# Column-major u, z and result, z's halves swapped by DMA, and a half chunk of keys held twice, in a TensorE-heavy attention and MLP kernel

## The chip, the cores and the metric

The kernel runs on one core of a Trainium2 chip. The metric is the device time of one execution in microseconds; a version is judged by the median of several runs. The profile comes from one execution of its own, recorded by the hardware profiler. Its span is shorter than the time of a run by what lies around it.

## What is computed

Two batches of 3008 rows go through an attention without softmax, and the 6016 rows of its result through two MLPs, one after the other:

```python
def _attn_ref(u, v, z):                     # u, v: [2, 3008, 256]; z: [2, 3008, 64]
    scores = (1.0 / S) * np.matmul(z, z.transpose(0, 2, 1))
    attn = np.maximum(scores, 0.0) ** 2
    return u * np.matmul(attn, v)

def _moe_ref(x, w_in, w_out, a, b):         # w_in: [256, 2048], w_out: [2048, 256]
    h = x @ w_in
    P = a[0] + a[1] * h + a[2] * h**2 + a[3] * h**3
    Q = 1.0 + np.abs(b[0]) * np.abs(h) + np.abs(b[1]) * h**2
    return (P / (Q + 1e-06)) @ w_out

def _moe2_ref(x, w_in, w_out, alpha):       # the same sizes
    h = x @ w_in
    return (np.maximum(h, 0.0) + alpha * np.minimum(h, 0.0)) @ w_out
```

## The kernel before

Products are made in float32 accuracy out of a narrower type, float32r: an operand is cut into a rounded part hi and a rest lo (`split`, line 92: a cast, then a subtraction on VectorE), and hi hi + hi lo + lo hi add up in PSUM. One product of 128 by 128 weights with 512 columns is thus three matmuls.

The 3008 rows of a batch are worked in six blocks of queries, five of 512 and one of 448, twelve blocks in all. Keys come in chunks of 128 partitions, two chunks to a pair, twelve pairs to a block; the last chunk has only 64 keys, and its other 64 partitions are zeros (line 108). Per block:

- `load_z` (line 204) loads 512 rows of z with rows on partitions, splits them on VectorE into a tile [hi | lo] (L96, L97), transposes its four chunks on TensorE (L214, tile zps) and copies the result on ScalarE (L216). That is zA: 64 partitions of hi above 64 of lo. `a_begin` (line 228) makes zB, the same with its halves swapped, by a product with a permutation matrix (L232, tile zbps) and a copy on ScalarE (L234). zA with zA gives hi hi + lo lo of a score, zA with zB gives the two mixed products (L250, L251).
- `a_scores` takes relu (L252) and square (L253) of a pair's scores on ScalarE, and splits them into ahi and alo. In the first block of all VectorE makes both parts, later ScalarE makes ahi.
- `a_values` and `pairs` (line 264) add a pair to the block's sum acca: eight matmuls move hi (v's two parts, two chunks, two halves of the 256 columns; L269), four move lo (L278). They come three pairs after the scores (LAG_A).
- `a_u` and `a_end`, behind a block's last pair: u's rows are loaded into a buffer (uraw), transposed by eight TensorE instructions (L304, tile ups), copied by ScalarE into ut (L307), multiplied with acca on VectorE (L313), and stored to DRAM as xd (L315).

The first MLP (`m1_*`) loads xd of a block (`load_x`, L320), splits it, and works through 2048 hidden units in eight steps of 256: `hidden` (L260 to L262), elementwise work, and `pairs` into acc1. Its result goes to DRAM as x2d (L403); the second MLP (`m2_*`) does the same with x2d. `m2_end` (line 436) copies the sum (L439), transposes it on TensorE (L447, tile ops; eight for a block), copies again (L451, L453) and stores (L455, L459).

What sets the order: 30 steps of attention alone, in which weights of the first MLP are loaded and decoded from float64 words by VectorE (`decode`, line 127); then attention with a share of the first MLP; from about 780 us the two MLPs without attention. The tile framework orders instructions by priorities and dependences, so an engine's list is not the text's order. Each engine works its list in order and waits at an instruction whose inputs are not there.

Shared places: all loads and stores of 4 KB per partition (zraw, vraw, wraw, uraw, ut, xr, x2, ot, o) take turns in two buffers (tag raw, RAW = 2). The tag s, two PSUM buffers, holds scores, the hidden units of the second MLP, and zps, zbps, ups and ops. The tag acc0 holds acca, and later the second MLP's sum. All of these loads and stores are issued by SP in one list (the DMA queue of SyncE; SPq in the rows). The second MLP's prepared weights are fetched by GpSimd's queue (w<-wd, L180), most of them about the end of attention.

## Time and profile before

| | us |
|---|---|
| median of 3 runs | 1631.24 |
| fastest and slowest of them | 1630.53, 1632.41 |
| span of the profiled execution | 1629.7 |
| TensorE matmuls busy | 1595.3 |
| TensorE weight loads busy (beside matmuls) | 1320.9 |
| VectorE busy | 1399.9 |
| ScalarE busy | 1222.4 |
| GpSimd busy | 28.5 |

Busy time of matmuls counts each from its start to its modelled end, and consecutive matmuls overlap. So a share near 98% says that TensorE nearly always has something under way, and what one matmul costs is read from the distance between two starts. The profile names PE for TensorE, PEld for its weight loads, DVE for VectorE, ACT for ScalarE, POOL for GpSimd and SP or SPq for SyncE's DMA queue; L250 is line 250 of the kernel.

### The profile page before, as it was taken

The page shows a single profiled execution, that of the slowest core. Times are in us where ns is not written, and L with a number is a line of the kernel's source. Part 1 is how long each engine was busy: PE and PEld are TensorE (multiplying, and loading weights), DVE is VectorE, ACT ScalarE, POOL GpSimd, SP SyncE. Part 2 cuts the span into 40 slices and gives each one's busy share as a digit, 9 for nine tenths or more (in the row PEclk, how much of TensorE's full clock was granted, in tenths as well). Part 3 has the DMA queues.
Part 4 walks back from the last instruction along what each step waited for, and adds up shares of the span by engine and source line. Part 5 has one row for each costly group of instructions (what it writes and reads, how often), then busy time and mean ns, then how long its engine had stood idle before and what let it go on. Part 6 is the DMA issues. An engine that isn't in the chain of part 4 may idle for free.

```text
span 1629.7 us, 18674 instructions
## 1 busy us (share of the span) xinstructions
PE 1595.3 (98%) x7164; PEld 1320.9 (81%) x7164; DVE 1399.9 (86%) x1498; ACT 1222.4 (75%) x1546; POOL 28.5 (2%) x57
## 2 busy tenths in 40 slices
PE   7899999999999999999899999999999999999998
PEld 5677888888888888888788888888888888888887
DVE  6998898988889888877799898898899989898863
ACT  5688898999989899988567666666666666666643
POOL 0000000000000000001000000000000000000000
PEclk9999999999999999999999999999999999999999
DMA  4323111221112120113400010101101010100000
GB/s 107 103 93 116 56 36 65 81 87 54 52 52 78 52 78 27 52 38 122 146 1 26 25 39 1 39 1 41 49 1 38 1 39 14 37 14 27 14 0 25
DMA packets 48169, 78.51 MB, mean 48 GB/s; under 512 B 9040, under 2 KB 28624, under 8 KB 48080
## 3 DMA queue, kind: packets, MB, share of 16 engines
q1 hardware_dynamic: 41056, 60.53, 11.5%
q0 software_dynamic: 7024, 16.79, 3.4%
q8 instruction: 56, 0.92, 0.2%
q14 instruction: 33, 0.27, 0.1%
HBM read 50.90 MB, written 26.41 MB: 47 GB/s over the span
## 4 chain that ended last, share of the span: by engine, by line
PE 89%; DVE 5%; DMA 2%; ACT 2%; issue 1%; SPq 0%; ACTq 0%; DVEq 0%
PE acc L269 20%; PE acca L269 13%; PE h L260 10%; PE h L261 10%; PE acc L278 10%; PE h L262 10%; PE acca L278 7%; PE s L250 3%; PE s L251 3%; DVE alo L97 1%; DMA vraw<-in_v_dram 1%; PE ops L447 1%; PE ups L304 1%; DMA xr<-xd 1%; DMA wraw<-in_moe_w_in_dram 0%
## 5 line engine op out<-in xcount | busy, mean ns | idle before, releaser
L269 PE MATMUL acc<-ghi,w 128*128 128x512 f32 (+1 forms) x1536 | 378.3, 386 | 0.0
L269 PEld LDWEIGHTS acc<-ghi,w 128*128 128x128 f32 x1536 | 287.7, 188 | 54.0 <-ACT ghi L94 0.3
L260 PE MATMUL h<-xhi,w 128*128 128x512 f32 (+1 forms) x768 | 298.6, 390 | 4.5 <-ACT xhi L94 4.5
L261 PE MATMUL h<-xlo,w 128*128 128x512 f32 (+1 forms) x768 | 297.3, 387 | 0.0
L262 PE MATMUL h<-xhi,w 128*128 128x512 f32 (+1 forms) x768 | 297.3, 387 | 0.0
L269 PE MATMUL acca<-ahi,vt 128*128 128x512 f32 (+1 forms) x1152 | 293.5, 387 | 1.3 <-DVE ut L313 1.1
L269 PEld LDWEIGHTS acca<-ahi,vt 128*128 128x128 f32 x1152 | 215.6, 188 | 44.7 <-DVE ut L313 3.0
L97 DVE TENSOR_TENSOR alo<-r,ahi 128x1024 fp32r<-128x1024 f32 (+1 forms) x144 | 172.6, 1199 | 59.4 <-PE acc L269 46.2
L420 ACT ACTIVATE m<-h,sal 128x512 f32<-128x512 f32 (+1 forms) x192 | 127.8, 680 | 110.7 <-PE h L262 110.1
L369 ACT ACTIVATE sq<-h 128x1024 f32<-128x1024 f32 (+1 forms) x96 | 97.0, 1010 | 141.5 <-PE h L262 139.6
L278 PE MATMUL acc<-glo,w 128*128 128x512 f32 (+1 forms) x768 | 202.8, 385 | 0.2 <-DVE glo L386 0.2
L260 PEld LDWEIGHTS h<-xhi,w 128*128 128x128 f32 x768 | 144.8, 189 | 34.5 <-ACT xhi L94 5.4
L97 DVE TENSOR_TENSOR glo<-m,ghi 128x1024 fp32r<-128x1024 f32 (+1 forms) x96 | 115.2, 1200 | 64.0 <-PE acc L269 48.5
L261 PEld LDWEIGHTS h<-xlo,w 128*128 128x128 f32 x768 | 144.9, 189 | 27.3 <-DVE xlo L97 0.7
L262 PEld LDWEIGHTS h<-xhi,w 128*128 128x128 f32 x768 | 144.9, 189 | 27.0
L278 PEld LDWEIGHTS acc<-glo,w 128*128 128x128 f32 x768 | 144.0, 188 | 27.7 <-DVE glo L386 1.0
L252 ACT ACTIVATE r<-s 128x512 f32<-128x512 f32 (+1 forms) x256 | 143.7, 592 | 23.9 <-DVE t L385 19.1
L421 DVE SCALAR_TENSOR_TENSOR m<-h,sg,m 128x512 f32<-128x512 f32 (+1 forms) x192 | 138.4, 735 | 18.9 <-ACT m L420 18.2
L278 PE MATMUL acca<-alo,vt 128*128 128x512 f32 (+1 forms) x576 | 154.2, 386 | 0.0
L253 ACT ACTIVATE r<-r 128x1024 f32<-128x1024 f32 (+1 forms) x144 | 151.5, 1053 | 2.1
L94 ACT CAST ahi<-r 128x1024 fp32r<-128x1024 f32 (+1 forms) x132 | 135.3, 1032 | 7.4 <-PE acca L278 6.5
L373 DVE SCALAR_TENSOR_TENSOR ab<-sq,cb,ab 128x1024 f32<-128x1024 f32 (+1 forms) x96 | 120.8, 1258 | 15.6 <-ACT ab L370 15.0
(83 smaller groups left out, 2164.2 us busy)
## 6 DMA issues: line engine op xcount, KB each, us to landing
wraw<-in_moe_w_in_dram SPq DMA_DIRECT2D x16, 512.0 KB, 3.7
wraw<-in_moe_w_out_dram SPq DMA_DIRECT2D x16, 512.0 KB, 3.6
wd<-dec POOLq DMA_DIRECT2D x32, 256.0 KB, 2.3
w<-wd POOLq DMA_DIRECT2D x16, 512.0 KB, 3.7
vraw<-in_v_dram SPq DMA_DIRECT2D x10, 512.0 KB, 3.9
uraw<-in_u_dram SPq DMA_DIRECT2D x10, 512.0 KB, 4.0
xd<-ut SPq DMA_DIRECT2D x10, 512.0 KB, 2.8
xr<-xd SPq DMA_DIRECT2D x10, 512.0 KB, 3.2
```

The costliest lines, as they stand in the source:

```text
L94: nc.scalar.copy(dst_hi, src)
L97: nc.vector.tensor_tensor(dst_lo, src, dst_hi.bitcast(F32), ALU.subtract)
L252: nc.scalar.activation(r[:, i, :n], s, AF.Relu, scale=1.0 / S)
L253: nc.scalar.activation(r[:, :, :n], r[:, :, :n], AF.Square)
L260: nc.tensor.matmul(acc, w_hi, hi, start=first, stop=False)
L261: nc.tensor.matmul(acc, w_hi, lo, start=False, stop=False)
L262: nc.tensor.matmul(acc, w_lo, hi, start=False, stop=last)
L269: nc.tensor.matmul(acc[:, e, :n], w[:, k, i, e * P : (e + 1) * P], hi[:, i, :n], start=first and i == 0 and k == 0, stop=False,)
L278: nc.tensor.matmul(acc[:, e, :n], w[:, 0, i, e * P : (e + 1) * P], lo[:, i, :n], start=False, stop=last and i == 1,)
L373: nc.vector.scalar_tensor_tensor(ab, sq, b1, ab, ALU.mult, ALU.add)
L420: nc.scalar.activation(t[:, i], h, AF.Copy, scale=sal[:, f : f + 1])
L421: nc.vector.scalar_tensor_tensor(t[:, i], h, sg[:, f : f + 1], t[:, i], ALU.mult, ALU.max)
```

## The change

The host lays out u as [256, 3008] for each batch, and z as [128, 3008], its 64 rows twice, one below the other. The result leaves the core as [256, 6016], and the host turns it back. Nothing is transposed on TensorE any more, and the identity and the permutation are gone.

`load_z` now gets z column-major: it rounds all 128 partitions into zA, and subtracts on the lower 64 only, in place, so that zA is hi above lo as before. For the first block zB is cut from the same load (ScalarE the lower half, VectorE the upper); for the others `a_begin` makes it by two SBUF-to-SBUF transfers of 64 partitions on SP's queue, which swap zA's halves. `a_u` is one load straight into ut, called once the second-last pair's products are written down. `m2_end` stores the copied sum as it is.

The last chunk of 64 keys is held twice over the partitions, in z's columns and in v's rows. For it the scores' hi stands on partitions 0 to 63 and their lo on 64 to 127 (two subtractions in the last pair); v's lo is set to zero on the lower half. So the passes that moved hi give hi hi + lo hi, and the third pass for this chunk, hi lo, is left out (`both` = 1): the two matmuls, one for each half of the columns.

```diff
+            for p0 in (0, HALF):
+                nc.sync.dma_start(
+                    out=t[p0 : p0 + rest, full, :], in_=src[r0 + full * P : r0 + n, :]
+                )
...
+            if kp + i == NKP - 1:
+
+                h2 = t[HALF:P, 0, 1].bitcast(F32)
+                nc.vector.tensor_tensor(t[HALF:P, 1, 1], h2, h2, ALU.subtract)
...
     def load_z(b, g):
-        """z's rows of one block as [hi; lo] over partitions, transposed."""
+
         raw = raw_tile("zraw")
-        r3 = raw[:, 0 : 4 * DQ].rearrange("p (c d) -> p c d", c=4)
-        load_rows(r3, z[b], g * QB, qn[g])
-        nch = -(-qn[g] // P)
-        zz = zp.tile([P, 4, P], F32R, tag="z", name="zz")
-        split(zz[:, 0:nch, 0:DQ], zz[:, 0:nch, DQ:P], r3[:, 0:nch, :], on_act=False)
-        ps = psw.tile([P, QB], F32, tag="s", bufs=2, name="zps")
-        for c in range(nch):
-            nc.tensor.transpose(ps[:, c * P : (c + 1) * P], zz[:, c, :].bitcast(F32), ident)
+        n = qn[g]
+        nc.sync.dma_start(out=raw[:, 0:n], in_=zt[b, :, g * QB : g * QB + n])
+        if n % P:
+            nc.sync.dma_start(out=raw[:, n : n + HALF], in_=zt[b, :, S - HALF : S])
+            n += HALF
         t = zp.tile([P, QB], F32R, tag="z", name="zA")
-        nc.scalar.copy(t[:, 0 : nch * P], ps[:, 0 : nch * P])
+        nc.vector.tensor_copy(t[:, 0:n], raw[:, 0:n])
+        if (b, g) == (0, 0):
+            zB[b, g] = zp.tile([P, QB], F32R, tag="z", name="zB")
+            nc.scalar.copy(zB[b, g][HALF:P, 0:n], raw[HALF:P, 0:n])
+            nc.vector.tensor_tensor(
+                zB[b, g][0:HALF, 0:n], raw[0:HALF, 0:n], t[0:HALF, 0:n].bitcast(F32), ALU.subtract
+            )
+        nc.vector.tensor_tensor(
+            t[HALF:P, 0:n], raw[HALF:P, 0:n], t[HALF:P, 0:n].bitcast(F32), ALU.subtract
+        )
         zA[b, g] = t
...
     def a_begin(b, j):
+
+        if (b, j) in zB:
+            return
         n = qn[j]
-        ps = psw.tile([P, QB], F32, tag="s", bufs=2, name="zbps")
-        nc.tensor.matmul(ps[:, :n], perm, zA[b, j][:, :n], start=True, stop=True)
         t = zp.tile([P, QB], F32R, tag="z", name="zB")
-        nc.scalar.copy(t[:, :n], ps[:, :n])
+        for p0 in (0, HALF):
+            nc.sync.dma_start(
+                out=t[p0 : p0 + HALF, :n].bitcast(F32),
+                in_=zA[b, j][HALF - p0 : P - p0, :n].bitcast(F32),
+            )
         zB[b, j] = t
...
+        on_act = (b, j) != (0, 0)
+        if kp < NKP - 1:
+            split(hi[:, :, :n], lo[:, :, :n], r[:, :, :n], on_act)
+        else:
+
+            if on_act:
+                nc.scalar.copy(hi[:, :, :n], r[:, :, :n])
+            else:
+                nc.vector.tensor_copy(hi[:, :, :n], r[:, :, :n])
+            for dst, rows, i in ((lo, slice(0, P), 0), (hi, slice(HALF, P), 1)):
+                nc.vector.tensor_tensor(
+                    dst[rows, i, :n], r[rows, i, :n], hi[rows, i, :n].bitcast(F32), ALU.subtract
+                )
...
-    def pairs(acc, w, hi, lo, n, first, last):
-        """acc += w^T (hi + lo) over a pair of chunks; what needs lo comes last."""
+    def pairs(acc, w, hi, lo, n, first, last, both=2):
...
-        for i in range(2):
+        for i in range(both):
...
-                    stop=last and i == 1,
+                    stop=last and i == both - 1,
...
-        pairs(acc, vk, hi, lo, n, kp == 0, kp == NKP - 1)
+        last = kp == NKP - 1
+        pairs(acc, vk, hi, lo, n, kp == 0, last, 1 if last else 2)
...
     def a_u(b, j):
         n = qn[j]
-        raw = raw_tile("uraw")
-        r3 = raw.rearrange("p (c d) -> p c d", c=4)
-        load_rows(r3, u[b], j * QB, n)
         t = tmp.tile([P, ND, QB], F32, tag="raw", name="ut", bufs=RAW)
-        for d in range(ND):
-            ps = psw.tile([P, QB], F32, tag="s", bufs=2, name="ups")
-            for c in range(-(-n // P)):
-                nc.tensor.transpose(
-                    ps[:, c * P : (c + 1) * P], r3[:, c, d * P : (d + 1) * P], ident
-                )
-            nc.scalar.copy(t[:, d, :n], ps[:, :n])
-        return t
+        nc.sync.dma_start(
+            out=t[:, :, :n],
+            in_=ut_in[b, :, j * QB : j * QB + n].rearrange("(e p) s -> p e s", p=P),
+        )
+        uts[b, j] = t
 
     def a_end(b, j):
         n = qn[j]
-        t = a_u(b, j)
+        t = uts.pop((b, j))
...
-        full, rest = divmod(n, P)
-        o = tmp.tile([P, 4, D], F32, tag="raw", name="o", bufs=RAW)
-        for g in range(0, full + (rest > 0), 2):
-            ps = psw.tile([P, 2, D], F32, tag="s", name="ops", bufs=2)
-            for c in range(g, min(g + 2, full + (rest > 0))):
-                m = P if c < full else rest
-                for e in range(ND):
-                    nc.tensor.transpose(
-                        ps[:m, c - g, e * P : (e + 1) * P], t[:, e, c * P : c * P + m], ident
-                    )
-            k = min(2, full - g)
-            nc.scalar.copy(o[:, g : g + k, :], ps[:, 0:k, :])
-            if g + 1 == full and rest:
-                nc.scalar.copy(o[:rest, full, :], ps[:rest, 1, :])
         r0 = b * S + j * QB
         nc.sync.dma_start(
-            out=out[r0 : r0 + full * P, :].rearrange("(c p) d -> p c d", p=P), in_=o[:, 0:full, :]
+            out=out[:, r0 : r0 + n].rearrange("(e p) s -> p e s", p=P), in_=t[:, :, :n]
         )
-        if rest:
-            nc.sync.dma_start(out=out[r0 + full * P : r0 + n, :], in_=o[:rest, full, :])
...
+                if kp == NKP - 2:
+                    a_u(*q)
...
-        a = _np.ascontiguousarray(inputs[name])
+        a = inputs[name]
+        if name == "u":
+            a = a.transpose(0, 2, 1)
+        if name == "z":
+            a = _np.concatenate([a, a], axis=2).transpose(0, 2, 1)
+        a = _np.ascontiguousarray(a)
...
-    return got[0]
+    return _np.ascontiguousarray(got[0].T)
```

TensorE's list at the start of the program, in the kernel before (s and sp are score tiles, zps and zbps as above, a number marks the buffer):

```order
L214 MATMUL zps_108<-ident_81,zz_105 128x128 x4
L232 MATMUL zbps_123<-zA_113,perm_86 128x512
L250 MATMUL sp_162<-zA_113 128x512
L251 MATMUL sp_162<-zB_125,zA_113 128x512
L214 MATMUL zps_132<-ident_81,zz_129 128x128 x4
L250 MATMUL s_148<-zA_113 128x512
L251 MATMUL s_148<-zB_125,zA_113 128x512
L250 MATMUL s_152<-zA_113 128x512
L251 MATMUL s_152<-zB_125,zA_113 128x512
```

The first score stands behind z's transposes and the permutation. The same place on TensorE in the changed kernel:

```order
L266 MATMUL s_125<-zA_97 128x512
L267 MATMUL s_125<-zB_99,zA_97 128x512
L266 MATMUL s_129<-zA_97 128x512
L267 MATMUL s_129<-zB_99,zA_97 128x512
L266 MATMUL sp_139<-zA_97 128x512
L267 MATMUL sp_139<-zB_99,zA_97 128x512
L266 MATMUL s_165<-zA_97,zA_113 128x512
L267 MATMUL s_165<-zB_99,zA_113 128x512
L266 MATMUL s_169<-zA_97,zA_113 128x512
```

The transposes and the permutation are gone from the head, and the scores of a second buffer come in their place.

SP's list of issues where attention ends, in the kernel before (xd0_5 is the attention result of the first batch's last block, x2d0_0 the first MLP's result of the first block, uraw and ut the last two blocks' u):

```order
L103 DMA uraw_6073<-in_u_dram 128x4x256
L403 DMA x2d0_3_5800<-x2_5798 128x1024
L103 DMA uraw_6512<-in_u_dram 128x3x256
L109 DMA uraw_6512<-in_u_dram 64x256
L315 DMA xd1_4_6089<-ut_6075 128x1024
L320 DMA xr_6586<-xd0_5_3332 128x2x448
L315 DMA xd1_5_6530<-ut_6516 256x1x448
L320 DMA xr_6638<-x2d0_0_2529 128x1024
```

The load of xd0_5 stands behind the last block's u in uraw. The same place on SP in the changed kernel:

```order
L327 DMA ut_5760<-in_u_dram 128x2x512
L426 DMA x2d0_3_5555<-x2_5553 128x1024
L327 DMA ut_6241<-in_u_dram 128x2x448
L338 DMA xd1_4_5829<-ut_5760 128x1024
L343 DMA xr_6310<-xd0_5_3146 128x2x448
L343 DMA xr_6362<-x2d0_0_2418 128x1024
L338 DMA xd1_5_6254<-ut_6241 256x1x448
```

The last block's u is one transfer into ut instead of two into uraw, and takes the place of one of the two load buffers until the product; the loads of xd0_5 and x2d0_0 stand behind it in both.

VectorE's list at the end of the first block, in the kernel before (dec and w are weights being decoded and split, alo the lo part of a pair's scores, ut the block's product):

```order
L139 SCALAR_TENSOR_TENSOR dec_599<-wraw_597,dec_599 128x512
L97 TENSOR_TENSOR w_564<-dec_556,w_564 128x512
L140 TENSOR_TENSOR dec_599<-dec_599 128x512
L97 TENSOR_TENSOR alo_620<-r_610,ahi_619 128x1024
L96 CAST w_607<-dec_599 128x512
L97 TENSOR_TENSOR alo_646<-r_635,ahi_645 128x1024
L97 TENSOR_TENSOR w_607<-dec_599,w_607 128x512
L313 TENSOR_TENSOR ut_663<-acca_221,ut_663 128x1024
```

Two alo of the next block stand shortly ahead of the product (L313), and a third farther up. The same place on VectorE in the changed kernel:

```order
L142 SCALAR_TENSOR_TENSOR dec_506<-wraw_504,dec_506 128x512
L136 TENSOR_SCALAR dec_548<-dec_548 128x512
L143 TENSOR_TENSOR dec_506<-dec_506 128x512
L139 SCALAR_TENSOR_TENSOR dec_548<-wraw_546,dec_548 128x512
L93 CAST w_514<-dec_506 128x512
L141 TENSOR_SCALAR dec_548<-dec_548 128x512
L94 TENSOR_TENSOR w_514<-dec_506,w_514 128x512
L142 SCALAR_TENSOR_TENSOR dec_548<-wraw_546,dec_548 128x512
L336 TENSOR_TENSOR ut_584<-acca_191,ut_584 128x1024
L143 TENSOR_TENSOR dec_548<-dec_548 128x512
L94 TENSOR_TENSOR alo_569<-r_559,ahi_568 128x1024
```

The two alo have moved behind the product (L336), and seven rows of decoding stand between the last reading of the load buffer by dec_506 (L142, the first row) and the product.

## Rows read from the trace of the kernel before

**Rows 1.** Page, parts 1 and 4: busy us, share, instructions; the chain's shares.

```profile
PE 1595.3 (98%) x7164; PEld 1320.9 (81%) x7164; DVE 1399.9 (86%) x1498; ACT 1222.4 (75%) x1546; POOL 28.5 (2%) x57
...
PE 89%; DVE 5%; DMA 2%; ACT 2%; issue 1%; SPq 0%; ACTq 0%; DVEq 0%
```

**Rows 2.** Windows: us, busy by engine (instructions), granted clock, DMA share, GB/s.

```profile
0.00:20.00 20.00, 8.59 (x26) 5.12 (x27) 7.79 (x20) 8.09 (x14) 3.04 (x9) 1.00 0.50 105
20.00:80.00 60.00, 53.21 (x222) 40.63 (x221) 56.62 (x95) 39.94 (x60) 0.00 (x0) 0.94 0.32 98
80.00:165.00 85.00, 80.24 (x348) 63.12 (x347) 74.50 (x115) 73.10 (x101) 1.09 (x2) 1.00 0.33 107
165.00:780.00 615.00, 614.79 (x2778) 507.43 (x2777) 532.68 (x544) 554.09 (x717) 23.86 (x45) 1.00 0.20 65
780.00:800.00 20.00, 15.52 (x59) 12.76 (x58) 11.09 (x12) 7.96 (x10) 0.53 (x1) 0.83 0.54 173
800.00:1560.00 760.00, 759.75 (x3433) 635.92 (x3433) 687.94 (x681) 510.53 (x607) 0.00 (x0) 1.00 0.07 22
```

**Rows 3.** Timeline, TensorE: start, us, line, tiles, count [idle before <- releaser].

```profile
82.88 1.98 PE L269 MATMUL acca<-ahi,vt 128*128 128x512 f32 x8
84.69 1.07 PE L278 MATMUL acca<-alo,vt 128*128 128x512 f32 x4
...
1588.00 1.09 PE L447 MATMUL ops<-ident,ot 128*128 128x128 f32 x8 [1.10 <-ACT ot L439]
1588.85 0.65 PE L269 MATMUL acc<-ghi,w 128*128 128x448 f32 x2
```

**Rows 4.** Groups by form: count | busy us, mean ns | idle before.

```profile
L304 PE MATMUL ups<-ident,uraw 128*128 128x128 f32 x96 | 13.7, 285 | 4.3 <-DMA uraw<-in_u_dram 4.3
```

**Rows 5.** Waits of TensorE: total us, times, longest.

```profile
PE zps L214 <- DVE zz L97: 7.6, 3, 4.7
...
PE ups L304 <- DMA uraw<-in_u_dram: 4.3, 2, 3.9
```

**Rows 6.** Timeline of the first block.

```profile
2.84 1.17 POOL L192 DMA_DIRECT2D al<-in_moe_alpha_dram  x1
...
12.63 0.80 PE L251 MATMUL sp<-zB,zA 128*128 128x512 f32 x1 [3.36 <-ACT zB L234]
...
26.84 1.22 DVE L97 TENSOR_TENSOR alo<-r,ahi 128x1024 fp32r<-128x1024 f32 x1
27.98 0.42 DVE L96 CAST vt<-vraw 128x512 fp32r<-128x512 f32 x1
...
78.29 1.22 DVE L313 TENSOR_TENSOR ut<-acca,ut 128x1024 f32<-128x1024 f32 x1
```

**Rows 7.** DMA issues: count, KB each, median us from issue to landing.

```profile
uraw<-in_u_dram SPq DMA_DIRECT2D x10, 512.0 KB, 4.0
...
al<-in_moe_alpha_dram POOLq DMA_DIRECT2D x1, 8.0 KB, 5.3
```

**Rows 8.** Timeline of the change of batches.

```profile
777.12 1.03 PE L304 MATMUL ups<-ident,uraw 128*128 128x128 f32 x8
...
778.18 0.59 SPq L320 DMA_DIRECT2D xr<-xd  x1
...
787.46 1.03 ACT L94 CAST xhi<-xr 128x448 fp32r<-128x448 f32 x2 [7.90 <-DMA xr<-xd]
...
793.48 1.59 PE L260 MATMUL h<-xhi,w 128*128 128x512 f32 x3 [4.48 <-ACT xhi L94]
...
794.88 0.57 PE L261 MATMUL h<-xlo,w 128*128 128x448 f32 x1
...
799.37 0.40 PE L262 MATMUL h<-xhi,w 128*128 128x512 f32 x1
```

**Rows 9.** Timeline of the end.

```profile
1623.34 0.91 ACT L439 COPY ot<-acc 128x896 f32<-128x896 f32 x1 [5.02 <-PE acc L278]
...
1626.34 0.50 SPq L459 DMA_DIRECT2D out_dram<-o  x1
```

More of the change, by code (lines that the diff above doesn't have):

```diff
@@ L6 @@
 from concourse._compat import with_exitstack
-from concourse.masks import make_identity
 F32 = mybir.dt.float32
@@ L39, in relu2_attention_rational_mlp_prelu_mlp @@
     tc: tile.TileContext,
-    u: bass.AP,
+    ut_in: bass.AP,
     v: bass.AP,
-    z: bass.AP,
+    zt: bass.AP,
     w1i: bass.AP,
@@ L55, in relu2_attention_rational_mlp_prelu_mlp @@
     P = 128
-    B, S, D = u.shape
-    DQ = z.shape[2]
+    B, S, D = v.shape
+    DQ = zt.shape[1] // 2
     F = w1i.shape[1]
@@ L65, in relu2_attention_rational_mlp_prelu_mlp @@
     NKP = NK // 2
+    HALF = P // 2
+    assert S % P == HALF and DQ == HALF
     assert ND == 2 and 2 * DQ == P and NK % 2 == 0 and NF % 2 == 0
@@ L107, in load_rows @@
         if rest:
-            nc.vector.memset(t[rest:P, full, :], 0.0)
-            nc.sync.dma_start(out=t[:rest, full, :], in_=src[r0 + full * P : r0 + n, :])
+            for p0 in (0, HALF):
+                nc.sync.dma_start(
+                    out=t[p0 : p0 + rest, full, :], in_=src[r0 + full * P : r0 + n, :]
+                )
     vt = {}
@@ L202, in relu2_attention_rational_mlp_prelu_mlp @@
     zA = {}
+    zB = {}
     def load_z(b, g):
         raw = raw_tile("zraw")
[L207 to L216 removed]
+        n = qn[g]
[3 more added lines that the diff above has]
+            n += HALF
+        t = zp.tile([P, QB], F32R, tag="z", name="zA")
+        nc.vector.tensor_copy(t[:, 0:n], raw[:, 0:n])
[8 more added lines that the diff above has]
+        )
         zA[b, g] = t
@@ L224, in relu2_attention_rational_mlp_prelu_mlp @@
     x2 = {}
-    zB = {}
+    uts = {}
     ahl = {}
@@ L577 @@
 _INS = ["u", "v", "z", "moe_w_in", "moe_w_out", "moe_a", "moe_b", "moe2_w_in", "moe2_w_out", "moe2_alpha"]
-_OUTS = [((6016, 256), "float32")]
+_OUTS = [((256, 6016), "float32")]
 def kernel(**inputs):
```

6 lines of the change are left out of this document (removed).

## The prediction

> **What bounds the kernel now.** I read the page first: TensorE is busy for 98% of the span and is 89% of the chain that ended last, VectorE is busy for 86% and is 5% of that chain [rows 1]. An average hides stages, so the table of windows comes next [rows 2]. From 165 to 780 us and from 800 to 1560 us TensorE's busy time is the window itself (614.79 of 615, 759.75 of 760): there nothing but TensorE's own work sets the pace. In the first 80 us it is not so: from 20 to 80 us VectorE is busy 56.62 of 60 us and TensorE 53.21. From 80 to 165 us TensorE has 4.8 us of gaps, and from 780 to 800 us it has 4.5, at a granted clock of 0.83.
>
> Busy time says nothing of a matmul's price, since matmuls overlap, so prices are read from one start to the next [rows 3]: eight 128x512 products take 84.69 - 82.88 = 1.81 us, 0.227 each, and eight 128x128 transposes 1588.85 - 1588.00 = 0.85, 0.106 each. A transpose shows 285 ns of its own in the grouped row [rows 4]; charging that would be nearly three times too much.
>
> **TensorE's removed work.** Per block the change takes out 8 transposes of u, 8 of the result and 4 of z, one permutation product and two lo products (the last chunk's lo pass, over two halves of the columns): in 12 blocks 240 x 0.106 = 25.4, 12 x 0.227 = 2.7 and 24 x 0.227 = 5.4, together 33.5 us. Not all of it lies where TensorE is the bound. Before 79.6 us stand 24 of z's transposes, two permutations, 8 transposes of u and two lo products: 3.4 + 0.9 = 4.3 us, which VectorE's pace hides. The last 8 transposes (0.85) lie behind the last product, and are counted with the tail. **Left: 28.3 us.** Below that it could be only if the pitch is not what the bound is; above it if the work before 79.6 us counted too (32.6).
>
> **The head.** The first score that needs both of z's forms starts at 12.63 us, after 3.36 us of waiting for ScalarE's zB [rows 6]; zB came out of a permutation on TensorE, whose matrix VectorE had to build first. TensorE's three waits for z's hi and lo parts, 7.6 us in all, are the largest entry of its table of waits [rows 5]. All of that goes for the first block: the order shows scores at the head of TensorE's list, with zA and zB cut straight from the load. What is late next is VectorE's sg, which stands in front of zA's last part and needs alpha. Alpha's load was issued at 2.84 us [rows 6] and 5.3 us is its time to landing [rows 7], so 8.1; the identity's two steps on GpSimd, gone now, come ahead of it, which gives back some 0.8. With a 512-column instruction behind it (half of alo's 1.22 us [rows 6], 0.6) the first score is at about 8.2 us: -4.4. The first block's end is paced by VectorE: from its fourth alo to its product is 78.29 - 26.84 = 51.45 us [rows 6], nearly all busy. In the new order one alo of the next block stands ahead of that product where three stood: -2 x 1.22, less 0.3 for zeroing v's last lo part (256 columns at alo's rate) and some for z's wider splits: -2.0. Sum -6.4, of which I take **-6**, since the weights' loads and the splits that follow could be late instead. Bounds: 0 (VectorE's list from the weights' first decode is the pace, and an earlier start only waits for them) and -10 (TensorE is busy 8.59 of the first 20 us [rows 2], so most of its 11.4 idle ones).
>
> ScalarE loses the copies of z, zB, u and the result. After the head no long wait of TensorE is for those copies, save the two for the result that are counted below: nothing.
>
> **What the DMA queue takes on.** z's halves are swapped by two SBUF-to-SBUF transfers a block on SP's queue. No row of before has such a transfer; its cost to TensorE lies between nothing and one 512 KB load's 4.0 us [rows 7] for each block that waits for it. The order has them ahead of the block by one to several weights' or u loads, so I take nothing after the head. Some of them wait for a z buffer that TensorE must free, with loads of weights and u queued behind on SP: that is where it would show. u now lands transposed, and its load follows the second-last pair's values; in the first block its buffer is free when VectorE has read the last word of a load of weights, seven rows ahead of the product in the order, and at 512 columns of alo's rate those take about 0.6 us each, 4 us, as long as the landing (4.0 by the same row): nothing, but with little to spare; once the first MLP's work lies between, there is more.
>
> At the same place the two new instructions on partitions 64 to 127 (z's lo, and the last pair's hi) stand among 128-partition ones. In the trace a VectorE instruction starts 0.08 us before the one ahead of it ends (26.84 + 1.22 = 28.06 against 27.98 [rows 6]). [...]
>
> **Stalls from 80 to 165 us.** 4.8 us of gaps [rows 2], some from u's load (4.3 in all, of which 3.9 before 80 us [rows 5]), most from products that wait for VectorE and scores that wait for PSUM. Transposes no longer take turns in the scores' two PSUM buffers. I take **-1.5**, a third; bounds -4.8 (all) and +4 (one late swap).
>
> **The change of batches, 780 to 800 us.** The last u load holds one of the two shared load buffers until TensorE transposes it at 777.12. Only then does SP issue xd's load, at 778.18; ScalarE sees it at 787.46 after 7.90 us, and TensorE, which needs the load queued behind it, waits 4.48 us until 793.48 [rows 8]. Then it runs at the lower of its two clock levels: twelve products from 794.88 to 799.37 take 0.374 us each, where 0.20 to 0.23 is the price at the full clock: 12 x 0.16 = 1.9, and 0.7 more for those just ahead. In the new order u's load is in a buffer that the product reads, nothing of TensorE's stands between, and xd's load waits only for a store's landing. **-4.5 - 2.6 = -7.1**; bounds 0 (the load is slow because weights' fills share the DMA engines, 0.54 busy in that window [rows 2], and that stays) and -9 (what is lost there and just after).
>
> **The second-last and last result.** At 1588 TensorE waited 1.10 us for the copy ahead of the transposes [rows 3]; in the order twelve products of the last hidden units now stand there: **-1.2**. At the end the copy starts at 1623.34 and the last store is issued at 1626.34 [rows 9], 3.4 us ahead of the end; now the store can be issued when the copy ends, at 1624.3. It is 448 KB where the last was 64, so I allow 3.9 to the end: 1628.2, **-1.5** (bounds 0 and -2).
>
> **Sum.** 28.3 + 6 + 1.5 + 7.1 + 1.2 + 1.5 = 45.6. The profiled execution took 1629.7; 1584.1 is the span to expect. The median of the runs, 1631.24, is 1.5 above: **1586**.
>
> **Rivals.**
> *The streaming goes and the rest stays.* If VectorE's list sets the head whatever the start, and the batch change stays slow because the fills share the DMA engines, only 28.3 + 1.2 + 1 are won: 1631.2 - 30.5 = 1601. For it: the DMA share, and VectorE's 56.62 of 60. Against it: the order, in which the blocked load no longer follows a transpose. 22%.
> *All stalls go.* Head -10, 80 to 165 us -4.8, batch change -9, tail -2: 28.3 + 10 + 4.8 + 9 + 1.2 + 2 = 55.3, 1576. For it: every wait named in the tables of TensorE has its cause removed. Against: VectorE has to do as much as before. 10%.
> *The products' streams are not the bound.* Weight loads are busy 1320.9 us (81%) [rows 1], so TensorE's 98% may be overlap counted as work; the removed matmuls would then cost nothing, and 45.6 - 28.3 = 17.3 would be left: 1614. Against: the next matmul starts 0.227 us after the last whatever comes, for hundreds in a row. [...] 4%.
> *Slower: the product waits for u.* The product stands in VectorE's list in order; if u's load, now issued late and behind a full queue, lands 4.0 us after VectorE reaches it, then alo's behind it are late and TensorE with them, 12 x 4.0 = 48 us, and each wait of that length brings the low clock's 2.6 us as at 794: 12 x 6.6 = 79. 1586 + 48 to 79 is 1634 to 1665. It decides from seven blocks at 6.6 us. Against: u's load needs only a free load buffer, and from the third block TensorE has the MLP's work between. 3%.
> The last 1% is for no difference (gains and such waits in balance).
>
> **How the numbers follow.** Forecast 60%, the rivals 22, 10, 4 and 3. The forecast's own bounds, with a miss of a few us in head, stalls or junction, run from 1577 to 1595. To leave no more than 2 in 10 out I reach up over the first rival and its misses, to 1604. About 0.2% (3.3 us) is what a measurement of this kernel can tell from no change: faster 0.96, within it 0.01, slower 0.03.
>
> **What would show it.** Right: starts of matmuls still 0.227 apart with no transposes between; the first score with zB at about 8 us; the first block's product at about 70 to 73 us; no wait of over 1 us and no low clock near 750 to 780 us; the last store right behind the copy. Wrong: SP waiting for TensorE with u loads behind it, a product of VectorE that waits for ut, scores that wait for zB's transfer, or the gap at the batch change in its old size.

## The result, and the profile after

The changed kernel takes 1588.29 us (median of 4 runs, 1587.83 to 1590.72) beside 1630.88 of the kernel before (4 runs): a ratio of 0.9745, with a 95% interval of 0.9731 to 0.9758. That is 42.6 us less. The forecast was 1586, in a range of 1577 to 1604. The profiled execution's span is 1586.2 us, where 1584.1 was expected.

The page after (parts 1 and 4), which answers to [rows 1]:

```profile
PE 1555.5 (98%) x6888; PEld 1288.9 (81%) x6888; DVE 1405.0 (89%) x1505; ACT 1183.9 (75%) x1473; POOL 28.1 (2%) x55
...
PE 89%; DVE 5%; ACT 3%; DMA 1%; issue 1%; POOL 0%; DVEq 0%; SPq 0%; ACTq 0%; POOLq 0%
```

TensorE is still busy for 98% of a shorter span and is still 89% of the chain. VectorE has 5 us more work in 43 us less time, and goes from 86% to 89%.

The windows after (us, then busy time and count by engine in the order PE, PEld, DVE, ACT, POOL; the granted clock, the DMA engines' share, GB/s), for [rows 2]. The change of batches now lies about 760 us:

```profile
0.00:20.00 20.00, 10.63 (x33) 8.04 (x34) 11.88 (x22) 10.84 (x17) 2.58 (x7) 1.00 0.45 118
20.00:80.00 60.00, 48.94 (x188) 35.48 (x187) 55.96 (x93) 32.07 (x48) 0.00 (x0) 0.95 0.45 132
80.00:165.00 85.00, 81.65 (x352) 64.92 (x351) 76.66 (x120) 74.53 (x102) 1.10 (x2) 1.00 0.35 105
165.00:780.00 615.00, 613.26 (x2717) 504.79 (x2716) 551.76 (x567) 545.40 (x695) 24.42 (x46) 1.00 0.24 75
740.00:760.00 20.00, 20.00 (x95) 17.48 (x94) 16.29 (x15) 13.47 (x17) 4.76 (x9) 1.00 0.63 207
760.00:780.00 20.00, 19.82 (x89) 16.40 (x89) 17.57 (x18) 12.51 (x14) 0.53 (x1) 1.00 0.40 137
```

From 740 to 780 us TensorE has no gap to speak of and its clock stays at 1.00; the 4.5 us of [rows 8] are gone. From 80 to 165 us its gaps fell from 4.8 to 3.4 us in this profile (a second profile of the same kernel, below, has 4.8). But from 165 to 780 us there are 1.7 us of gaps where 0.2 stood, and from 20 to 80 us it is busy for 48.94 us, less than the 53.21 before, while VectorE is as full as it was (55.96 us, 56.62 before).

TensorE's waits after (us in total, times, longest), for [rows 5]:

```profile
PE s L266 <- DVE zA L225: 9.3, 2, 8.4
PE acca L297 <- DVE ut L336: 5.5, 2, 3.2
...
PE acca L306 <- DVE alo L94: 2.6, 3, 1.5
```

The pitch of its products (timeline of TensorE after, as [rows 3]):

```profile
762.05 2.00 PE L297 MATMUL acc<-ghi,w 128*128 128x512 f32 x8
763.89 1.07 PE L306 MATMUL acc<-glo,w 128*128 128x512 f32 x4
```

Eight products take 763.89 - 762.05 = 1.84 us, 0.23 each: the price of a product did not move when the transposes around it went. Of the old waits, for z's transposes and for u's load, none is left. In their place stand waits for VectorE: zA's second half at the start, the product with u at the ends of the first two blocks, and alo. The waits for ScalarE's relu grow as well, to 6.1 us in all from 3.7.

Where the time went is read from the starts of the same instructions in the two traces. The second and third row of the table rest on these starts, before (timelines of VectorE and ScalarE):

```profile
782.02 1.09 DVE L313 TENSOR_TENSOR ut<-acca,ut 128x896 f32<-128x896 f32 x1 [1.70 <-issue]
...
879.20 1.02 ACT L439 COPY ot<-acc 128x1024 f32<-128x1024 f32 x1 [1.04 <-PE acc L278]
```

and after:

```profile
761.79 1.09 DVE L336 TENSOR_TENSOR ut<-acca,ut 128x896 f32<-128x896 f32 x1 [0.85 <-PE acca L306]
...
850.42 1.02 ACT L462 COPY ot<-acc 128x1024 f32<-128x1024 f32 x1 [1.04 <-PE acc L306]
```

| up to | before | after | won in this stage | forecast |
|---|---|---|---|---|
| first block's product with u | 78.29 | 75.04 | 3.2 | 6 |
| last block's product with u | 782.02 | 761.79 | 17.0 | 20.6 |
| first copy of a result | 879.20 | 850.42 | 8.6 | 7.1 |
| last copy of a result | 1623.34 | 1581.43 | 13.1 | 10.5 |
| end of the span | 1629.74 | 1586.25 | 1.6 | 1.5 |
| sum | | | 43.5 | 45.7 |

(The forecast's 28.3 us of matmuls are put where they stood: 112 transposes, 10 permutations and 22 lo products in the second row, 19.1, with 1.5 for the stalls; 88 transposes in the fourth, 9.3, with 1.2 for the wait.) The sum is right to 2 us, and in part by luck: the first two rows brought 6.4 us less than forecast, the others 4.2 more. The runs below go after the rows.

The start of the changed kernel (timeline; SPq is SyncE's DMA queue), for [rows 6]:

```profile
7.45 0.17 DVE L198 TENSOR_SCALAR sg<-al 128x16 f32<-128x16 f32 x1 [2.79 <-DMA al<-in_moe_alpha_dram]
7.66 0.69 DVE L225 TENSOR_TENSOR zA<-zraw,zA 64x512 fp32r<-64x512 f32 x1
...
8.40 0.80 PE L266 MATMUL s<-zA 128*128 128x512 f32 x1 [8.40 <-DVE zA L225]
8.43 0.34 SPq L213 DMA_DIRECT2D zraw<-in_z_dram  x1
...
8.99 0.63 PE L267 MATMUL s<-zB,zA 128*128 128x512 f32 x1
```

VectorE's fourth alo, one of its gaps and the first product in the same trace (timeline, VectorE):

```profile
23.84 1.22 DVE L94 TENSOR_TENSOR alo<-r,ahi 128x1024 fp32r<-128x1024 f32 x1
...
31.60 0.43 DVE L136 TENSOR_SCALAR dec<-dec 128x512 int32<-128x512 int32 x1 [0.70 <-ACT dec L134]
...
75.04 1.23 DVE L336 TENSOR_TENSOR ut<-acca,ut 128x1024 f32<-128x1024 f32 x1 [0.32 <-DMA ut<-in_u_dram]
```

And the product on TensorE that waited for it (timeline, TensorE):

```profile
76.32 0.97 PE L297 MATMUL acca<-ahi,vt 128*128 128x512 f32 x3 [3.17 <-DVE ut L336]
```

The first score starts at 8.40 us, 0.2 from the forecast. The first with zB, whose start of 12.63 the forecast counted from, stands right behind it at 8.99: that is 3.6 us sooner, not 4.4. The first score waits for zA's second half at 7.66, which stands behind sg, which waits 2.79 us for alpha. The instruction at 7.66 is also the last reader of z's load buffer, and the second load of z is issued right behind it, at 8.43. Before, that load went out at 4.61 us. The fourth alo comes 3.0 us earlier than before, not 3.6. From there to the product it is 51.2 us, where 51.45 stood: the 2.0 us of the two missing alo did not come. VectorE's instructions in between, the product included, do sum to 2.1 us less (53.0 for 55.1). But its gaps are 4.0 us for 2.9, and its instructions overlap by 4.6 us for 5.3. Three times, as at 31.60, the next instruction in its list waits 0.70 us for a step of the decoding that ScalarE does, and the product waits 0.32 us for u's load.

VectorE about the end of the first block (timeline, VectorE alone):

```profile
66.32 0.69 DVE L282 TENSOR_TENSOR alo<-r,ahi 128x512 fp32r<-128x512 f32 x1
67.02 0.69 DVE L282 TENSOR_TENSOR ahi<-r,ahi 64x512 fp32r<-64x512 f32 x1
67.74 0.43 DVE L136 TENSOR_SCALAR dec<-dec 128x512 int32<-128x512 int32 x1
68.08 1.22 DVE L94 TENSOR_TENSOR alo<-r,ahi 128x1024 fp32r<-128x1024 f32 x1
69.22 0.68 DVE L139 SCALAR_TENSOR_TENSOR dec<-wraw,dec 128x512 int32<-128x512 int32 x1
```

Here the overlap of instructions is seen: 67.74 to 68.08 is 0.09 us shorter than the first instruction's 0.43, and 68.08 to 69.22 is 0.08 shorter than 1.22. But the subtraction on partitions 64 to 127 (67.02) starts 0.70 us after the one ahead of it, and the next 0.72 after it, with 0.69 each: no overlap at either end. No run here tells the start at partition 64 from the smaller number of partitions. Between the fourth alo and the product five such instructions stand; at 0.08 us twice for each, an estimate from the overlaps of this trace, they would lose 0.8 us, and 0.7 of overlap (5.3 less 4.6) are lost there. What such instructions cost in the whole kernel is measured by no run.

The end (timeline):

```profile
1581.43 0.91 ACT L462 COPY ot<-acc 128x896 f32<-128x896 f32 x1 [4.96 <-PE acc L306]
1582.36 0.37 SPq L464 DMA_DIRECT2D out_dram<-ot  x1
```

The store is issued 0.93 us behind the start of the copy, where 3.00 stood [rows 9], and the span ends 3.9 us after the issue, as allowed.

### The profile page after: what moved, and what is told of

It reads as the page before. It is cut to its first block, busy times and chain, and to the rows that moved or that the text cites. A ratio compares the mean times of both kernels' runs of the same rounds, so it can differ in the third digit from the quotient of the medians.

```text
span 1586.2 us, 18045 instructions
## 1 busy us (share of the span) xinstructions
PE 1555.5 (98%) x6888; PEld 1288.9 (81%) x6888; DVE 1405.0 (89%) x1505; ACT 1183.9 (75%) x1473; POOL 28.1 (2%) x55
## 4 chain that ended last, share of the span: by engine, by line
PE 89%; DVE 5%; ACT 3%; DMA 1%; issue 1%; POOL 0%; DVEq 0%; SPq 0%; ACTq 0%; POOLq 0%
PE acc L297 21%; PE acca L297 13%; PE h L288 11%; PE h L289 10%; PE acc L306 10%; PE h L290 10%; PE acca L306 6%; PE s L266 3%; PE s L267 3%; DVE alo L94 1%; ACT r L269 1%; ACT r L268 1%; ACT ahi L91 0%; DMA zraw<-in_z_dram 0%; DVE ahi L93 0%
## 5 line engine op out<-in xcount | busy, mean ns | idle before, releaser
L94 DVE TENSOR_TENSOR alo<-r,ahi 128x1024 fp32r<-128x1024 f32 (+1 forms) x132 | 158.1, 1199 | 36.0 <-PE acc L297 18.5
L306 PE MATMUL acca<-alo,vt 128*128 128x512 f32 (+1 forms) x552 | 150.6, 389 | 2.6 <-DVE alo L94 2.6
L406 DVE SCALAR_TENSOR_TENSOR ghi<-t,sc,sq 128x1024 fp32r<-128x1024 f32 (+1 forms) x96 | 120.9, 1259 | 10.8 <-ACT sq L402 5.6
```

The lines of the kernel that those rows point to most:

```text
L94: nc.vector.tensor_tensor(dst_lo, src, dst_hi.bitcast(F32), ALU.subtract)
L306: nc.tensor.matmul(acc[:, e, :n], w[:, 0, i, e * P : (e + 1) * P], lo[:, i, :n], start=False, stop=last and i == both - 1,)
L406: nc.vector.scalar_tensor_tensor(hi, t, a0, sq, ALU.add, ALU.mult)
```

## The experiments

All times are medians. The kernel before had 1630.9 us beside the first four kernels, 1630.2 beside the next seven and 1629.9 beside the last; the changed kernel, run again beside three of them, 1589.07 us. The base of the later runs, 1586.92, comes from another chip than they do; the kernel before took 1630.24 us on its chip and 1630.18 on theirs.

### The result alone

The kernel before with the change's `m2_end` and nothing else:

```diff
-        full, rest = divmod(n, P)
-        o = tmp.tile([P, 4, D], F32, tag="raw", name="o", bufs=RAW)
...
-            out=out[r0 : r0 + full * P, :].rearrange("(c p) d -> p c d", p=P), in_=o[:, 0:full, :]
+            out=out[:, r0 : r0 + n].rearrange("(e p) s -> p e s", p=P), in_=t[:, :, :n]
```

> The kernel before with one part of the change alone: the result stored column-major, so m2_end is one copy and one store, and the 96 transposes of the result with their second copies are gone. Theory (the distance from start to start is the price): 88 transposes ahead of the last product x 0.106 = 9.3, the wait of 1.2 at the second-last result, 1.5 at the end: 12.0, so 1618.9 from the median of 1630.9. Rival (matmul busy time is overlap, the streams cost nothing): only the two waits, 2.7, so 1628.2.

Measured: 1616.19, a ratio of 0.9913 (0.9898 to 0.9928): 14.7 us won, more than the 12.0 of the theory and far from the rival's 2.7. The size is read from the copies of two results, the fourth and the eleventh. In the kernel before (timeline, ScalarE):

```profile
1098.90 1.01 ACT L439 COPY ot<-acc 128x1024 f32<-128x1024 f32 x1 [0.95 <-PE acc L278]
...
1586.93 1.01 ACT L439 COPY ot<-acc 128x1024 f32<-128x1024 f32 x1 [0.40 <-PE acc L278]
```

In this run (the same view):

```profile
1094.23 1.02 ACT L439 COPY ot<-acc 128x1024 f32<-128x1024 f32 x1 [0.95 <-PE acc L278]
...
1574.83 1.01 ACT L439 COPY ot<-acc 128x1024 f32<-128x1024 f32 x1 [0.41 <-PE acc L278]
```

488.03 us lie between them before and 480.60 here, 7.43 less for seven results: 1.06 us each, where eight times 0.106 is 0.85. The kernel before shows the rest at the seam of any such group (timeline, TensorE):

```profile
1022.34 0.39 PE L261 MATMUL h<-xlo,w 128*128 128x512 f32 x1
1022.70 1.09 PE L447 MATMUL ops<-ident,ot 128*128 128x128 f32 x8
1023.55 0.47 PE L262 MATMUL h<-xhi,w 128*128 128x512 f32 x1
1023.86 0.39 PE L260 MATMUL h<-xhi,w 128*128 128x512 f32 x1
```

The eight transposes take 0.85 us, but the first starts 0.36 us after the product ahead, not 0.227, and the product behind them takes 0.31: 0.13 + 0.85 + 0.08 = 1.06.

### u alone

The kernel before with the change's `a_u`, called behind the second-last pair:

```diff
-        raw = raw_tile("uraw")
...
+        nc.sync.dma_start(
+            out=t[:, :, :n],
+            in_=ut_in[b, :, j * QB : j * QB + n].rearrange("(e p) s -> p e s", p=P),
+        )
```

> The kernel before with u alone column-major: one load straight into ut behind the second-last pair, no transposes of u. Theory: 88 transposes behind the first block x 0.106 = 9.3, and the gap at the change of batches with its low clock, 7.1, goes because no load buffer waits for TensorE: 16.4, plus up to 1 of stalls, so about 1614. Rival (the load of xd is late because the weights' fills share the DMA engines): the gap stays and 9.3 to 10 are won, 1621. Second rival (the product waits for a late u): under 9.

Measured: 1612.20, 0.9888 (0.9872 to 0.9905): 18.7 us won. Up to the last product with u it is 10.7 us, at the change of batches 7.8 more, and nothing later. The windows about that place:

```profile
765.00:785.00 20.00, 20.00 (x93) 17.03 (x92) 17.07 (x17) 10.64 (x13) 2.06 (x4) 1.00 0.63 200
780.00:800.00 20.00, 19.64 (x87) 15.59 (x86) 19.57 (x20) 14.14 (x17) 0.00 (x0) 1.00 0.07 29
```

The DMA engines are no less busy from 765 to 785 us than in the gap before, 0.63 for 0.54 [rows 2], and TensorE is busy all the time at clock 1.00. So the weights' fills do not make that gap.

### One buffer moved

The kernel before, with its transposes, and u's last load in a weights' buffer:

```diff
+    def u_early(b, j):
+        raw = big.tile([P, 2, 2, D], F32R, tag="big", name="uraw")
+        r3 = raw.rearrange("p a c d -> p (a c) d").bitcast(F32)
+        load_rows(r3, u[b], j * QB, qn[j])
+        early[b, j] = r3
...
+                if q == blocks[-1] and kp == LAG_A:
+                    u_early(b, j)
```

> The kernel before with one buffer moved: u's rows for the last block are loaded into one of the weights' buffers that the values have given back, early in that block, and no longer into one of the two shared load buffers; all transposes stay. Theory (the gap at 780 to 800 us is the load of xd waiting for the buffer that u's transposes hold): the wait of 4.5 us and the low clock go, 7 us, so 1624. Rival (weights' fills on the DMA engines make the load late): no change, 1631, with the gap in its old place.

Measured: 1625.20, 0.9968 (0.9956 to 0.9979): 5.7 us won of 7. The queue's wait in the kernel before, between 765 and 800 us (waits of SP: us in total, times, longest):

```profile
SPq L320 <- PE ups L304: 47.3, 1, 47.3
```

This run's window at the place:

```profile
780.00:800.00 20.00, 19.42 (x86) 15.60 (x85) 16.30 (x18) 14.08 (x17) 0.53 (x1) 1.00 0.53 179
```

ScalarE's first reading of xd in this run (timeline):

```profile
779.68 1.04 ACT L94 CAST xhi<-xr 128x448 fp32r<-128x448 f32 x2
```

SP stood 47.3 us before the load of xd, until TensorE had transposed u. With that buffer elsewhere xd is read at 779.68 and not at 787.46 [rows 8], and from 780 to 800 us TensorE is busy for 19.42 us at clock 1.00, where it was 15.52 at 0.83, with the DMA engines as busy as then (0.53). The theory is shown: a shared buffer, held by a step of TensorE, was the gap. The first copy of a result comes 6.2 us earlier than before.

### z alone

> The kernel before with z alone column-major: the load of z, zA and zB by VectorE and by swapping transfers as in the changed kernel; u, the result and the three passes of the last half chunk stay as before (zeros in its 64 missing keys). Theory: 24 transposes x 0.106 = 2.5 and 10 permutations x 0.227 = 2.3 behind the first block, and the head's gain of about 3 as in the whole change: 8, so 1623. Rival (the swapping transfers delay the loads behind them on the queue): the gain is under 4, 1627 or more, and TensorE's waits name zB.

The edit is the change's `load_z` and `a_begin` without the last half chunk's second copy (its 64 missing keys are zeros). Measured: 1627.28, 0.9977 (0.9967 to 0.9987): 3.6 us won, less than half of the theory's 8. By its profile the first product comes 1.9 us earlier and the last 4.6, so 2.7 lie between them where the theory had 4.8. Over 2 us more are won at the change of batches: the first copy of a result comes 7.2 us earlier, and the span is 6.8 shorter. No wait of TensorE names zB, so the rival's number came without its sign. But TensorE's gaps from 165 to 760 us are 2.1 us in this run where the kernel before has 0.2: nearly all of what is missing between the two products. The change of batches still has a gap: TensorE waits 3.0 us there for the first xhi.

The profiled execution took 1624.6 us, 2.7 less than the median; what the median has lost beyond it is not in this trace and stays open.

### Three passes again

The changed kernel with the last half chunk as it was before. Its missing keys are zeros again in z and v, and its scores are split like any pair's; of the edit the line with the third pass:

```diff
-        pairs(acc, vk, hi, lo, n, kp == 0, last, 1 if last else 2)
+        pairs(acc, vk, hi, lo, n, kp == 0, last)
```

> The changed kernel with the last half chunk back in three passes: its 64 missing keys are zeros again in z and v, ahi and alo are split as for any pair, and the third pass covers both chunks. Theory (start-to-start price): 22 products behind the first block x 0.227 = 5.0, two more in the first block hidden by VectorE: 1593.3 against 1588.3. Rival (they hide under weight loads or VectorE): no change, 1588. VectorE has one instruction less per block, worth at most 0.3 in the head.

Measured: 1592.53, beside 1589.07 of the changed kernel: 3.5 us for the theory's 5.0. The products do cost time; a third of their price is not seen in the total. The windows show a place for it: from 80 to 780 us TensorE's gaps are 3.4 us in this run and 6.5 in the changed kernel beside it, so part of what was put back stands where TensorE waited.

### The swap undone

The changed kernel with the permutation product in `a_begin`:

```diff
-        for p0 in (0, HALF):
-            nc.sync.dma_start(
...
+        ps = psw.tile([P, QB], F32, tag="s", bufs=2, name="zbps")
+        nc.tensor.matmul(ps[:, :n], perm, zA[b, j][:, :n], start=True, stop=True)
```

> The changed kernel with zB made as before, by the permutation product on TensorE and a copy on ScalarE, in place of the two swapping transfers; the first block's zB stays cut from the load. Theory (the transfers cost TensorE nothing): 11 products x 0.227 = 2.5 more, 1590.8. Rival (the transfers in SP's list hold up loads that matter): it gains back what they cost, 1588 or less.

Measured: 1588.51, no slower than the 1589.07 beside it. But two things had changed. The identity for the permutation occupies GpSimd ahead of alpha's load; alpha's instructions on VectorE then stand farther down, and the first score starts at 5.73 us and not at 8.4. The next pair of runs took that difference away.

### The changed kernel again

> The changed kernel once more, on the chip of the three runs beside it, as their base: 1588.3 within 1.5.

Measured: 1589.07 (1588.60 to 1589.64), within the 1.5 us expected. Its profile shows by how much a second execution can differ. From 80 to 165 us the gaps are as long as in the kernel before, 4.8 us (window):

```profile
80.00:165.00 85.00, 80.25 (x345) 63.32 (x345) 76.54 (x119) 74.03 (x101) 1.10 (x2) 1.00 0.35 105
```

### Alpha's instructions on GpSimd

```diff
-    nc.vector.tensor_scalar(sg, al, 1.0, -2.0, ALU.is_gt, ALU.mult)
+    nc.gpsimd.tensor_scalar(sg, al, 1.0, -2.0, ALU.is_gt, ALU.mult)
```

and likewise the two behind it.

> The changed kernel with the three small instructions on alpha (sg, sal) moved from VectorE to GpSimd; everything else as it is. Theory (the first score waits for zA's second half, which stands behind sg in VectorE's list, and the second load of z waits for the same instruction to give its buffer back): first score at 4.7 instead of 8.4 us, the chain of loads that takes turns in two buffers earlier by 2 to 3 us, the first block's product at 72 to 73 instead of 75.0: 1585.8. Rival (VectorE's list of splits and decoding is the pace, an earlier start only waits in front of it): first score at 4.7, product still at 75, 1588.3.

Measured: 1586.92, 2.1 us less than the 1589.07 beside it, each median outside the other's runs. The first score of this run (timeline, TensorE):

```profile
5.48 0.79 PE L266 MATMUL s<-zA 128*128 128x512 f32 x1 [5.48 <-DVE zA L225]
```

Its first product with u (timeline, VectorE):

```profile
71.74 1.23 DVE L336 TENSOR_TENSOR ut<-acca,ut 128x1024 f32<-128x1024 f32 x1 [0.36 <-DMA ut<-in_u_dram]
```

The first score comes 2.9 us earlier, the first product 3.3 (75.04 after). So an earlier start is carried through the whole first block; the rival, that it would only wait before VectorE's list, falls. By the third block's product 2.1 us of it are left.

### The swap undone, on that base

The two edits together: alpha's instructions on GpSimd, and the permutation in place of the swap. The identity is now made on GpSimd behind the issue of alpha's load.

> The changed kernel with alpha's instructions on GpSimd and zB made by the permutation on TensorE; it differs from the run with alpha's instructions on GpSimd (1586.9) by the swap alone, since the first score no longer waits for alpha in either. Theory (the swapping transfers are free): 11 products x 0.227 = 2.5 more, 1589.4. Rival (they hold up loads that share SP's list, which is why z alone and the run with the permutation both came out 2 to 4 us off): 1587 or less, and the difference lies between the first block and 780 us, at the waits of TensorE around the first blocks' ends.

Measured: 1588.52, 1.6 us more than 1586.92; by the spans of the two profiles 2.0 (1586.8 and 1584.8). If the 11 products cost their 2.5 us, the transfers cost between nothing and 0.9. What disturbs the view is the order: with the permutation the first product stands behind two alo of the next block again and starts at 75.83, 4.1 us later than in the base; TensorE waits for it for 6.6 us in one piece, where the base has 5.2 in two. By the fourth block's product 2.5 of the 4.1 us are left. The transfers are seen between 165 and 780 us (windows), in the base

```profile
165.00:780.00 615.00, 613.32 (x2716) 504.44 (x2715) 552.02 (x567) 544.23 (x694) 24.50 (x46) 1.00 0.24 75
```

and in this run

```profile
165.00:780.00 615.00, 614.20 (x2722) 505.70 (x2721) 552.79 (x567) 551.50 (x706) 24.42 (x46) 1.00 0.23 73
```

TensorE's gaps there are 1.7 us with the swap and 0.8 without; the first pair, without alpha's edit, shows 1.8 and 0.8. So the rival is right in kind: about 0.9 us of these gaps come with the swap. In the changed kernel SP stands for 36.5 us in all at the swaps (waits of SP), until TensorE is done with a z buffer, with loads queued behind. How much of the first block's difference belongs to the swap was not separated.

### ScalarE's casts in the first block

```diff
-        on_act = (b, j) != (0, 0)
+        on_act = True
```

> The changed kernel with alpha's instructions on GpSimd, and in the first block ScalarE instead of VectorE makes ahi (12 casts of 0.69 us on VectorE, 1.03 each on ScalarE). Theory (the first block is paced by VectorE's list): 12 x 0.69 = 8.3 us leave that list, its first product comes 4 to 8 us earlier than 71.7, the whole at 1580 to 1583. Rival (the loads' chain through two buffers, with the weights' decoding, is the pace): product within 1.5 us of 71.7, 1586.

Measured: 1583.84, 3.1 us less than its base of 1586.92. The first product of this run (timeline, VectorE):

```profile
66.83 1.23 DVE L336 TENSOR_TENSOR ut<-acca,ut 128x1024 f32<-128x1024 f32 x1
```

Its window from 20 to 80 us (columns as above):

```profile
20.00:80.00 60.00, 51.04 (x208) 37.01 (x207) 54.70 (x91) 44.89 (x64) 0.00 (x0) 1.00 0.48 141
```

4.9 us earlier at the product, inside the 4 to 8 of the theory; the whole, forecast at 1580 to 1583, misses by 0.8. The first block is paced by VectorE's list, and the clock is not the reason: in the second profile of the changed kernel it was 1.00 from 20 to 80 us too, with the product at 75.48. VectorE is still busy for 54.7 of the 60 us, with the next work; ScalarE takes 44.9 instead of 29.7, and has the room.

### The product first

```diff
-        nc.vector.tensor_tensor(t[:, :, :n], acc_a[b, j][:, :, :n], t[:, :, :n], ALU.mult)
+        with tc.high_priority(EARLY):
+            nc.vector.tensor_tensor(t[:, :, :n], acc_a[b, j][:, :, :n], t[:, :, :n], ALU.mult)
```

> The changed kernel with alpha's instructions on GpSimd, and the block's product with u given a higher priority on VectorE, so that it passes decoding and splits that stand ahead of it. Theory (TensorE's 5.5 us of waits for that product at the ends of the first two blocks come from its place in VectorE's list): 2 to 4 us less than 1586.9, 1584. Rival (VectorE has to do the same work before the next block's splits anyway): 1587.

Measured: 1585.43 (1583.60 to 1587.32, which reaches over the base's 1586.58 to 1587.60): 1.5 us, under the theory's 2 to 4. The sign of the theory isn't there either. The first product of this run (timeline, VectorE):

```profile
72.20 1.23 DVE L337 TENSOR_TENSOR ut<-acca,ut 128x1024 f32<-128x1024 f32 x1 [0.36 <-DMA ut<-in_u_dram]
```

TensorE waits for a swap once in this run (waits of TensorE):

```profile
PE s L267 <- DMA zB<-zA: 0.5, 1, 0.5
```

The first product is no earlier, and the waits for it, 5.2 in the base, are 4.9. But the theory was hardly put to the test: in VectorE's list the product stands behind the same seven rows of decoding as in the base in the first block, and passes one row of 0.42 us in the second. And in the first block its place alone could bring nothing, since it waits for u's load: that is issued at 68.45, when VectorE has read the last of the weights whose buffer it takes, and the product starts 3.75 us later. In the changed kernel it is 3.71 (71.33 to 75.04). Where the 1.5 us were won is not shown; the order of the first MLP's work differs from the third block on.

### The three together

> The changed kernel with alpha's instructions on GpSimd, ScalarE making ahi in the first block, and the product at a higher priority: the three edits that each gained by their profile. If the gains of the last two (1586.9 to 1583.8, and 1586.9 to 1585.4) are independent: 1582.3, with the first block's product near 67 us. If the product's priority only shifted the same work: 1583.8 or more.

Measured: 1583.77 (1581.44 to 1584.83), as with ScalarE's casts alone: the priority adds nothing. The first product is at 68.74. Two edits on top of the change, alpha's instructions on GpSimd and the casts on ScalarE, are thus the best version found: 1583.84, 0.9715 of the kernel before (0.9700 to 0.9729).

## Why the prediction came out right, step by step

**What bounds the kernel.** Right. The pitch of 0.227 stayed (0.23 after), and removed matmuls paid. The rival that matmul time is overlap gave 1614 for the whole and 1628 for the result alone; 1588 and 1616 were measured. The weight loads' share of the span is 81% before and after, and alone would not have told of the 42.6 us.

**TensorE's removed work.** Right in kind, mis-sized in two terms of opposite sign. A group of eight transposes was priced at 0.85 us from its first start to the start behind it; its two seams were left out. Measured on the result it is 1.06, so the fourth row of the table won 13.1 and not 10.5. The lo products were priced at 5.0 and gave 3.5 when put back, z's transposes and permutations at 4.8 and gave 2.7 alone, as gaps opened behind them.

**The head.** The step that failed: -6 forecast, -3.2 measured, and the sign of a first product at 70 to 73 us was missed (75.04). The reason that was given for the start, alpha ahead of zA, was right. Of the 6.4 us that were added up, 3.2 did not come. First, 0.8 at the start: 8.2 us came out for the first score (8.40), but the score with zB, counted from 12.63, is the next one (8.99). Second, 0.6 up to the fourth alo: the subtraction behind the instruction that waits for alpha also holds z's load buffer, so that the loads behind start later than before. Third, 1.8 from there to the product: the sum of rows ahead of it, which fell by 2.1 as counted, is not yet a time, and 1.1 us of gaps and 0.7 of lost overlap took nearly all of it. That VectorE paces the block was right: 8.3 us of casts taken off its list brought the product 4.9 us forward. It does so up to the last reading of the load buffer that u's load takes; from there, in the changed kernel, the load's 3.7 us set the product. The reason given for the bound of 0, "an earlier start only waits", falls with alpha's run.

**Swaps and u's load.** Taken at nothing; the swaps cost 0 to 0.9 us, and they show where the prediction said they would, in SP's waits for TensorE and in about half of the gaps between 165 and 780 us. u's load costs a wait of 0.3 us: the seven rows took 3.4 us and the landing 3.7, where 4 were forecast for each, so "nothing, but with little to spare" was the right price. The slower rival, a product that waits for u in each block, shows that one wait.

**Stalls from 80 to 165 us.** -1.5 forecast, -1.4 in one profile of the changed kernel and nothing in the other: the term is not shown. The gaps of 1.7 us between 165 and 780 us were not foreseen; of TensorE's waits there 0.9 us are for VectorE, 0.7 of them for alo, and 0.8 for ScalarE. With the swap undone 0.8 us of gaps are left, so half of them are the swap's; where the other half comes from was not tried.

**The change of batches.** -7.1 forecast, 8.6 measured in its row, and some of that may be work of the first MLP that moved across the row above. The reason is shown by itself: one buffer moved wins 5.7, and the low clock goes with the gap. In the trace of the kernel before the granted clock is 0.50 or 1.00 and takes no third value (the 0.83 of [rows 2] is the mean of its window): 0.50 from 794 to 799 us, where the products are 0.374 us apart, and 1.00 from 800 to 1560 us; with the buffer moved it is 1.00 from 780 to 800 us. The rival, the fills on the DMA engines, falls.

**The last results.** -1.2 and -1.5: the wait at the second-last result has gone, and the end is 1.6 shorter.

The four parts alone sum to 14.7 + 18.7 + 3.6 + 3.5 = 40.5, beside 41.2 for the whole on the chip of the second set: the sum gives no sign of a large effect of one part on another.

## What to carry to other kernels

Where one engine's work fills the window, price a removed instruction from the start of the one ahead to the start of the one behind its group, seams included: for the result's groups this was won in full, for the last chunk's lo products two thirds of it, since TensorE waits for other engines in part of that time. Where another engine paces, count also what it has at hand and which shared buffer each of its instructions holds: a wait for an 8 KB load cost 2 us there, and the cure was to move three small instructions to an engine that was busy for 2% of the span (GpSimd). A gap at a change of stages is first looked for in the DMA queue's waits: a load held up for 47 us by a buffer reads there in one line, though only 5.7 us of them were to be won.

## What was not expected of the hardware

A swap of 64 partitions within SBUF landed no sooner than four times as many bytes from memory (DMA issues after: count, KB each, median us from issue to landing):

```profile
ut<-in_u_dram SPq DMA_DIRECT2D x10, 512.0 KB, 3.7
...
zB<-zA SPq DMA_DIRECT2D x18, 128.0 KB, 4.1
```

4.1 us for 128 KB against 3.7 for 512. The swaps' time varies, from 2.1 to 6.3 us in this trace, and with z alone their median is 3.2. It is hidden here because zB is made ahead of its block; only in the two runs with the product first does TensorE wait for one, 0.5 and 0.6 us. And a group of eight transposes among wide products cost 0.2 us more than its own pitch, 0.13 ahead of it and 0.08 behind.
